# Attention with two matmul layers behind it: each pass over a pair of heads loads its own queries

## The chip, the cores and the metric

The kernel runs on one core of a Trainium2 chip. The metric is the device time of one execution in microseconds; the median of three runs before the change is 1149.49 us (1148.93 to 1151.54).

## The reference

Thirty-two heads (batch 4, 8 heads each) of 576 queries and keys with 64 features; every row of scores is cut at its maximum less tau before the exponent. Two layers over 2304 tokens follow, 512 to 2048 to 512 features each. All products are wanted in fp32; the weights arrive in 64 bits.

```python
scores = (q @ k.T) / 8
thresh = scores.max(-1) - tau
scores = where(scores >= thresh, scores, -1e9)
attn   = exp(scores - scores.max(-1))
x = (attn / (attn.sum(-1) + 1e-9)) @ v       # heads side by side: 2304 x 512
h = x @ w_in;  g = where(h >= 1, h, where(h <= -1, 0, (h + 1)**2 / 4));  y = g @ w_out
h = y @ w2_in; g = s * maximum(h, 0)**2 + b;                             out = g @ w2_out
```

## The kernel before

**Attention.** Two heads make a pair, and each pair is gone over twice. A unit is one pass: `half_` 0 takes the queries 0 to 255 in two tiles of 128, `half_` 1 the queries 256 to 575 in two tiles of 128 and a mixed tile, which holds the last 64 queries of both heads. There are 4 x 4 x 2 = 32 units. `prep` (line 389) loads queries and keys of the pair into a tile r (line 393, 128 rows of 1280 columns, 640 KB) and its values into vr (line 394), and scales all 640 columns of queries on POOL, VectorE or ACT (lines 397 to 399). Two tiles r and two vr take turns; the load for unit u+1 is added after the first query tile of the last part of unit u, and may start once the scores of unit u-1 have been computed.

For a query tile, `scores` (lines 424, 430) makes the products, VectorE finds the minimum of the negated scores (473), ACT takes the exponent (476), VectorE masks and sums (482), POOL or ACT normalises (518, 523), TensorE transposes in blocks (544, 558), ACT or VectorE evicts them to PT and PL (536, 537), and `av` (580, 581) multiplies by the values. Its result is split into a high and a low part, XH and XL (589, 592), and stored to xT (595). XH and XL exist twice; block q (256 tokens for even q, 320 for odd) uses number q % 2. The first 8 units compute the scores of one head at a time, the later ones of both heads together.

**The layers.** 16 slices f of 128 hidden features. A hidden tile is 12 matmuls (line 794), its outputs 12 more (837 in the attention stage, 880 and 914 afterwards). While attention runs, the layer's first slices are computed beside it for blocks 0 to 5: `FB[q]` slices for block q (`beside`, line 851). The rest of layer 1 and layer 2 follow when attention is over. Weights come in chunks of 128 x 256 (line 709, 256 KB each), and are turned from 64 bits into a high and a low part by ACT, VectorE and POOL (lines 712 to 725).

**The order of the work** is drawn by a planner, `Sched`, while the program is built. Every step is a task with the engines that can do it, their assumed durations, a priority, and keys that it reads and writes. `run` plays the tasks through: an engine that is free takes the ready task of the first priority; of two engines the one that is done sooner takes it, with a `PENALTY` on VectorE. A load is assumed to land after a time made of `DMA_ISSUE`, `DMA_RATE` and `DMA_LAG`. When TensorE has nothing ready, the planner puts in a fill matmul (line 986), whose product nobody reads. The order drawn so is fixed in the instruction queues; on the chip each engine and SP work through their queues in it, and wait on semaphores.

Attention steps get priorities (0, n) in the order in which they are added, shifted by `OFF[step]`; there are 304 numbers. Work of the layers comes behind, (1, n). The attention stage's weights stand among the attention steps, at W0 + WS * i, where i counts 20 parts (10 slices, each with an input and an output part).

```python
    f0, i = 0, 0
    for f1 in sorted(set(FB) | {F1}):
        for part in range(2):
            for f in range(f0, f1):
                weights(w1, f, (0, W0 + WS * i), (part,), 0)
                i += 1
        f0 = f1
```

In layer 1's last part the second layer's weights are loaded slice by slice as places come free, at least `PACE` slices apart.

Of the kernel before, what the change touches and what calls it, by code (L numbers as in the profile page):

```python
# [7 lines left out]
F32 = mybir.dt.float32  # L8
# [14 lines left out]
NWT = 4  # L23
TWO_PASS = 4

FB = [4, 8, 10, 10, 10, 10]
NA1 = len(FB)
PACE = 3
W0 = 40.0
WS = 5.75  # L30

WT0, WT = 0.0, 310.0

OFF = {"load": 0.0, "prep": 0, "qk": -6.0, "min": -3.0, "exp": -1.0, "mask": 0, "norm": 3.0, "trans": 3.58, "hi": 4.39, "av": 5.75, "xo": 0.0}
NSX, NSL, NR, NV = 4, 5, 2, 2
WARM = 9
# [5 lines left out]

QW, KW = 640, 640

ALONE = 6

APART = 8
DMA_ISSUE, DMA_RATE, DMA_LAG = 475, 360.0, 910.0
SCALE = 0.125

TINY, HUGE = 2.0 ** -15, 122880.0 - 2.0 ** -7

# [34 lines left out]
class Sched:  # L87
# [5 lines left out]
    CHANGE = 85.0  # L93
    PENALTY = {"dve": 1.5, "act": 0.3, "pool": 0.0}

# [53 lines left out]
    def run(self):  # L149
# [27 lines left out]
        while left:  # L177
# [4 lines left out]
            for d in batch:  # L182
                if d is None:
                    continue
                if d.group is not None:
                    d.group.left -= 1
                    if d.group.left == 0:
                        for b in d.group.banks:
                            bank_free[b] = None
                for s in d.succ:  # L190
                    s.preds.append((d.fn[0], now))
                    s.ready = max(s.ready, now)
                    s.npred -= 1
                    if s.npred == 0:
                        release(s)
            for e in engines:
# [7 lines left out]
                while q:  # L204
                    item = heapq.heappop(q)
                    t = self.tasks[item[1]]
                    if t.start is not None:
                        continue
                    g = t.group
                    if g is not None and g.banks is None:  # L210
                        pick = next((c for c in g.cands if all(bank_free.get(b) is None for b in c)), None)
                        if pick is None:
                            held.append(item)
                            continue
                        g.banks = pick
                        for b in pick:
                            bank_free[b] = g
# [24 lines left out]
                for item in held:  # L242
                    heapq.heappush(q, item)
                if e == "pe" and busy[e] <= now < self.fill_until:

                    b = next((b for b in self.fill_banks if bank_free.get(b) is None), None)
                    if b is not None:
# [3 lines left out]
                        t.fn = ("pe", self.fill_ns, self.fill(b))  # L251
                        bank_free[b] = t.group
                        busy[e] = array.run(now, self.fill_ns)
# [29 lines left out]
def pfast_ns(n):  # L283
    return 60 + 1.07 * n
# [20 lines left out]
def attention_then_ffn(tc, qk, v, tau, w1, w2, s2, b2, out):  # L305
# [77 lines left out]
    def at(pr, step):  # L383
        return pr[0], pr[1] + OFF[step]

    def load_const(key, dst, src, pr):
        add([("sp", DMA_ISSUE, lambda: nc.sync.dma_start(out=dst, in_=src.to_broadcast([128, 1])))], pr, w=[key], lag=512)

    def prep(u, b, pair):

        pr = prio_a()
        r, kr, vr, kvr = R[u % NR], ("R", u % NR), VR[u % NV], ("VR", u % NV)
# [4 lines left out]
        add([("pool", pfast_ns(QW), lambda: nc.gpsimd.tensor_scalar(out=q, in0=q, scalar1=-SCALE, scalar2=1.0, op0=ALU.mult, op1=ALU.mult)),  # L397
             ("dve", fast_ns(QW), lambda: nc.vector.tensor_scalar(out=q, in0=q, scalar1=-SCALE, scalar2=None, op0=ALU.mult), True),
             ("act", act_ns(QW), lambda: nc.scalar.activation(out=q, in_=q, func=AF.Copy, scale=-SCALE))],
            at(pr, "prep"), w=[kr])  # L400

    def both_tt(n, o, x, y, op):
# [6 lines left out]
    def scores(u, blk, hs):  # L409
# [6 lines left out]
        else:  # L416
            g = Group([(0, 1), (2, 3)] + [(6, 7)] * (u < ALONE))
        col = 0 if mixed else 128 + 128 * blk

        def qkmm():  # L420
            for x in range(2):
                if mixed:
                    k0 = QW + 64 + x * HS
                    nc.tensor.matmul(PS[g.banks[0]][:, x, 0:HS], r[:, col:col + 128], r[:, k0:k0 + HS], start=True, stop=True)  # L424
                    continue
                for i, h in enumerate(hs):
                    rows = slice(64 * h, 64 * h + 64)

                    k0 = QW + (0 if h else 64) + x * HS
                    nc.tensor.matmul(PS[g.banks[0] + 2 * i][:, x, 0:HS], r[rows, col:col + 128], r[rows, k0:k0 + HS], start=True, stop=True)  # L430
# [5 lines left out]
    def qtiles(u, blk):  # L436
# [94 lines left out]
        for x in range(nx):  # L531
            blocks_of_keys(pr, p, kp[2 * x], 0 if not x else S + 64, x, mixed, blk)
        last_keys(pr, p, kp[1], mixed, blk)

# [3 lines left out]

    def blocks_of_keys(pr, p, kp, c0, x, mixed, blk):
        g = Group([(4,), (5,)])  # L540
# [4 lines left out]

        add([("pe", 109 * 4, trans)], at(pr, "trans"), r=[kp], w=[("bank", g)], group=g)

# [4 lines left out]
        dst = PT[:, :, :, 512:S].rearrange("p s k c -> p k s c") if mixed else PT[:, x, :, blk * 128:blk * 128 + 128]  # L552
        evict(512, pr, [dst], src, [("bank", g)], [("PT", i, blk) for i in ((0, 1) if mixed else (x,))], g)

    def last_keys(pr, p, kp, mixed, blk):

        g = Group([(4,), (5,)])
        add([("pe", 109, lambda: nc.tensor.transpose(bank[g.banks[0]][:, 0:128], p[:, 512:640], ident))], at(pr, "trans"), r=[kp], w=[("bank", g)], group=g)  # L558

# [39 lines left out]

    units = [(b, pair, half_) for b in range(B) for half_ in ((0, 1) if b < TWO_PASS else (2,)) for pair in range(H // 2)]  # L600
    nxt = [0]

    def prep_next():
        if nxt[0] < len(units):
            prep(nxt[0], *units[nxt[0]][0:2])
            nxt[0] += 1
# [25 lines left out]
    def attention():  # L632
        prep_next()
        warm_up()
        load_const("tau", tau_c, tau, (0, 1.5))
        load_const("sb", s_c, s2, (0, 50))
# [185 lines left out]
    def a1_out(q, dm, slots):  # L822
# [4 lines left out]
        for half_ in range(2):  # L827
# [176 lines left out]
def _lay(inputs):  # L1004
    import numpy as np
    q, k, v = inputs["q"], inputs["k"], inputs["v"]
    qk = np.zeros((B, H, D, QW + KW), q.dtype)
    qt, kt = q.transpose(0, 1, 3, 2), k.transpose(0, 1, 3, 2)
    qk[:, 0::2, :, 0:64] = qt[:, 0::2, :, 512:]
    qk[:, 1::2, :, 64:128] = qt[:, 1::2, :, 512:]  # L1010
    qk[:, :, :, 128:QW] = qt[:, :, :, :512]
    qk[:, :, :, QW + 64:] = kt
    qk[:, 1::2, :, QW:QW + 64] = kt[:, 1::2, :, 512:]
    qk = qk.reshape(B, H // 2, 128, QW + KW)
    vp = np.zeros((B, H // 2, 128, 8 * D + 128), v.dtype)
# [36 lines left out]
```

## Time and profile before

| | us |
|---|---|
| median of three runs | 1149.49 |
| the profiled execution, its own time | 1148.21 |
| its span | 1146.4 |
| TensorE busy in the span | 1120.4 |
| VectorE, ACT, POOL busy | 621.4, 667.3, 542.8 |

The span runs from the first to the last instruction; the execution's own time holds 1.8 us around it. PE is TensorE's matmuls, PEld its weight loads, which overlap them. Matmuls are pipelined and their ends are modelled, so a busy PE need not be PE at its peak. The attention stage lies at 0 to 498 us, the rest of layer 1 up to 742 us, layer 2 behind it.

### The profile page before, as it was taken

The numbers are of one execution on the slowest core, as the hardware profiler recorded it, in microseconds if no ns is written. First come the engines' busy times: TensorE is split into PE (matmuls) and PEld (weight loads), VectorE is DVE, ScalarE is ACT, GpSimd is POOL, SyncE is SP. The second block draws the span as 40 slices with busy tenths as digits, with TensorE's granted clock in tenths as the row PEclk, the third lists the DMA queues.
The fourth block names the chain that finished last, engine by engine and source line by source line (L and its number), as shares of the span: only waits on it lengthen the run. The fifth ranks groups of instructions, "written<-read, shape, count | busy, mean of one in ns | idle before, by whom it ended". The sixth has DMA issues, their size and how long they took to land.

```text
span 1146.4 us, 21026 instructions
## 1 busy us (share of the span) xinstructions
PE 1120.4 (98%) x7608; PEld 976.1 (85%) x7608; DVE 621.4 (54%) x1519; ACT 667.3 (58%) x1538; POOL 542.8 (47%) x833
## 2 busy tenths in 40 slices
PE   9999989999999999999999999999999999999998
PEld 6667777777877788799999999999999999999997
DVE  6887877767756667548778875782111111111111
ACT  5887866757646656446665655565444444444443
POOL 4465565434434335347777765774323323233222
PEclk9999999999999999999999999999999999999999
DMA  4544634233222332145445765421001011000000
GB/s 161 171 129 151 185 112 128 70 104 118 94 69 88 110 103 74 53 138 165 146 155 178 234 193 177 135 87 38 19 19 37 3 36 38 1 19 20 1 19 19
DMA packets 66633, 108.86 MB, mean 95 GB/s; under 512 B 6368, under 2 KB 39648, under 8 KB 66528
## 3 DMA queue, kind: packets, MB, share of 16 engines
q1 hardware_dynamic: 66528, 107.50, 29.8%
q8 instruction: 60, 0.98, 0.3%
q14 instruction: 45, 0.37, 0.1%
HBM read 83.89 MB, written 23.59 MB: 94 GB/s over the span
## 4 chain that ended last, share of the span: by engine, by line
PE 82%; DMA 7%; DVE 4%; ACT 3%; POOL 1%; issue 1%; SPq 0%; ACTq 0%; DVEq 0%; POOLq 0%
PE ps L794 30%; PE ps L914 18%; PE ps L880 9%; PE ps L430 6%; PE ps L837 6%; PE ps L580 5%; PE ps L544 5%; DMA r<-in_qk_dram 4%; DMA st<-in_w_dram 3%; PE ps L581 2%; PE ps L424 1%; DVE p L482 1%; PE ps L558 1%; DVE hs L806 1%; PE ps L986 1%
## 5 line engine op out<-in xcount | busy, mean ns | idle before, releaser
L815 POOL TENSOR_TENSOR g<-hs,g 128x256 fp32r<-128x256 f32 (+1 forms) x272 | 214.0, 787 | 309.4 <-ACT g L814 287.7
L794 PE MATMUL ps<-xh,wh 128*128 128x256 f32 (+1 forms) x1088 | 317.8, 292 | 0.3 <-DVE hs L806 0.3
L794 PE MATMUL ps<-xl,wh 128*128 128x256 f32 (+1 forms) x1088 | 313.1, 288 | 0.0
L794 PE MATMUL ps<-xh,wl 128*128 128x256 f32 (+1 forms) x1088 | 312.9, 288 | 0.0
L812 DVE TENSOR_SCALAR hs<-c,s,b 128x256 f32<-128x256 f32 x144 | 65.2, 453 | 309.3 <-ACT c L811 309.3
L794 PEld LDWEIGHTS ps<-xh,wh 128*128 128x128 f32 x1088 | 206.0, 189 | 9.1 <-DVE stt L507 0.8
L794 PEld LDWEIGHTS ps<-xl,wh 128*128 128x128 f32 x1088 | 205.9, 189 | 6.2
L794 PEld LDWEIGHTS ps<-xh,wl 128*128 128x128 f32 x1088 | 205.8, 189 | 0.0
L914 PE MATMUL ps<-wh,g 128*128 128x512 f32 x576 | 203.2, 394 | 0.0
L814 ACT CAST g<-hs 128x256 fp32r<-128x256 f32 (+1 forms) x272 | 113.6, 418 | 94.9 <-DVE hs L812 62.8
L482 DVE SCALAR_TENSOR_TENSOR p<-ps,stt,e 128x576 f32<-128x576 f32 x144 | 115.5, 813 | 40.6 <-ACT e L476 21.4
L518 POOL TENSOR_SCALAR p<-p,stt 128x576 f32<-128x576 f32 (+1 forms) x124 | 98.2, 797 | 77.0 <-DVE stt L507 70.1
L809 ACT ACTIVATE hs<-ps 128x256 f32<-128x256 f32 x144 | 55.4, 385 | 132.3 <-PE ps L794 131.5
L473 DVE TENSOR_REDUCE stt<-ps 128x1 f32<-128x576 f32 x144 | 104.2, 750 | 48.7 <-PE ps L430 41.9
L403 POOL TENSOR_TENSOR wl<-wt,wh 128x256 fp32r<-128x256 f32 x128 | 101.5, 798 | 53.4 <-ACT wh L724 52.3
L914 PEld LDWEIGHTS ps<-wh,g 128*128 128x128 f32 x576 | 108.6, 189 | 19.5
L880 PE MATMUL ps<-g,wh 128*128 128x256 f32 (+1 forms) x608 | 122.7, 294 | 0.9 <-DVE ye L890 0.9
L476 ACT ACTIVATE e<-ps,stt 128x576 f32<-128x576 f32 x144 | 103.5, 744 | 32.9 <-DVE stt L473 30.7
L914 PE MATMUL ps<-wl,g 128*128 128x512 f32 x288 | 113.9, 395 | 0.0
L430 PE MATMUL ps<-r 64*128 64x288 f32 x512 | 98.3, 429 | 2.5 <-DVE p L482 2.3
L880 PEld LDWEIGHTS ps<-g,wh 128*128 128x128 f32 x608 | 97.3, 189 | 1.7 <-DVE ye L890 1.4
L804 ACT ACTIVATE c<-c,half 128x256 f32<-128x256 f32 (+1 forms) x128 | 68.6, 536 | 51.5 <-DVE c L802 49.5
(65 smaller groups left out, 1825.8 us busy)
## 6 DMA issues: line engine op xcount, KB each, us to landing
st<-in_w_dram SPq DMA_DIRECT2D x128, 256.0 KB, 3.6
r<-in_qk_dram SPq DMA_DIRECT2D x32, 640.0 KB, 4.4
vr<-in_v_dram SPq DMA_DIRECT2D x32, 320.0 KB, 3.3
xr<-xT SPq DMA_DIRECT2D x8, 640.0 KB, 6.1
xr<-y1T SPq DMA_DIRECT2D x9, 512.0 KB, 3.8
out_dram<-yo SPq DMA_DIRECT2D x18, 256.0 KB, 2.0
xr<-xT SPq DMA_DIRECT2D x8, 512.0 KB, 4.9
xT<-xh SPq DMA_DIRECT2D x16, 160.0 KB, 3.2
```

The lines of the kernel that those rows point to most:

```text
L403: return [("pool", pool_ns(n), lambda: nc.gpsimd.tensor_tensor(out=o(), in0=x(), in1=y(), op=op)), ("dve", dve_ns(n), lambda: nc.vector.te ...
L430: nc.tensor.matmul(PS[g.banks[0] + 2 * i][:, x, 0:HS], r[rows, col:col + 128], r[rows, k0:k0 + HS], start=True, stop=True)
L473: add([("dve", 665, lambda: nc.vector.tensor_reduce(out=nm[:, x:x + 1], in_=Sv(), axis=AX.XY, op=ALU.min))], at(pr, "min"), r=[kg], w=[ks[ ...
L476: add([("act", 624, lambda: nc.scalar.activation(out=ev, in_=Sv(), func=AF.Exp, bias=nm[:, x:x + 1], scale=-1.0))], at(pr, "exp"), r=[kg, ...
L482: nc.vector.scalar_tensor_tensor(out=p[:, x * S:x * S + S].rearrange("p (a c) -> p a c", a=2), in0=Sv(), scalar=nthr[:, x:x + 1], in1=ev, ...
L518: eng.tensor_scalar(out=p[:, o:o + w], in0=p[:, a:a + w], scalar1=rc[:, x:x + 1], scalar2=un[:, x:x + 1], op0=ALU.mult, op1=ALU.add)
L794: nc.tensor.matmul(o, a, x, start=(n == 0), stop=(n == 11))
L814: add([("act", act_ns(T), lambda: nc.scalar.copy(out=gh, in_=hs))], fp, r=[khs], w=kgh)
L815: add([("pool", pool_ns(T), lambda: nc.gpsimd.tensor_tensor(out=gl, in0=hs, in1=gh.bitcast(F32), op=ALU.subtract)), ("dve", dve_ns(T), lam ...
L837: nc.tensor.matmul(o, a[:, c], x, start=(f == 0 and n == 0), stop=(f == nf - 1 and n == 2))
L880: nc.tensor.matmul(o, a[:, c], x, start=(f == f0 and n == 0), stop=(f == f1 - 1 and n == 2))
L914: nc.tensor.matmul(o, x[:, c], a[:, 512:1024], start=(f == 0 and n == 0), stop=(f == NF - 1 and n == 2))
```

## The change

Each pass loads only its queries and the keys. In DRAM the pair lies as queries 0 to 255, keys, then the mixed tile's and the other queries; pass 0 takes the columns 0 to 895 (448 KB), pass 1 the columns 256 to 1279 (512 KB), and scales 256 or 384 columns of queries. Three tiles r of 1024 columns take turns instead of two of 1280; the values, in a function of their own and with a priority of their own, stay with two tiles. With that the attention has 336 priority numbers. `TWO_PASS` goes, which already named all batches, and `AHEAD = 1` adds no load.

In the planner: loads are assumed to land later, a bank counts as free only when TensorE could have heard of it, VectorE's penalty is 2.0, scores are drawn earlier and the normalisation too. Transposes of the first six units wait in the plan for their place in PT or PL, and the output sums beside attention follow one another. Fewer slices stand beside blocks 0 and 1, weights come 8 apart, the second layer's 5.

```diff
-FB = [4, 8, 10, 10, 10, 10]
+FB = [3, 7, 10, 10, 10, 10]
-PACE = 3
+PACE = 5
-WS = 5.75
+WS = 8.0
-OFF = {"load": 0.0, "prep": 0, "qk": -6.0, "min": -3.0, "exp": -1.0, "mask": 0, "norm": 3.0, ...}
+OFF = {"load": 0.0, "prep": 0, "qk": -8.0, "min": -3.0, "exp": -1.0, "mask": 0, "norm": 0.0, ...}
-NSX, NSL, NR, NV = 4, 5, 2, 2
+NSX, NSL, NR, NV = 4, 5, 3, 2
-QW, KW = 640, 640
+KW = 640
+PASS = ((0, 256 + KW), (256, KW + 384))
+KEYS, QUERIES = (256, 0), ((0, 256), (KW, KW + 384))
-DMA_ISSUE, DMA_RATE, DMA_LAG = 475, 360.0, 910.0
+DMA_ISSUE, DMA_RATE, DMA_LAG = 475, 350.0, 2500.0
-    PENALTY = {"dve": 1.5, "act": 0.3, "pool": 0.0}
+    PENALTY = {"dve": 2.0, "act": 0.3, "pool": 0.0}
...
+                        heard = now + self.HOP.get((d.fn[0], "pe"), 0)
                         for b in d.group.banks:
-                            bank_free[b] = None
+                            bank_free[b] = heard
...
-                        dma_free = max(dma_free, now + 1125.0) + t.lag / DMA_RATE
+                        dma_free = max(dma_free, now + 1400.0) + t.lag / DMA_RATE
...
-    R = [ap_.tile([128, QW + KW], F32, name=f"r{i}") for i in range(NR)]
+    R = [ap_.tile([128, 384 + KW], F32, name=f"r{i}") for i in range(NR)]
...
-    def prep(u, b, pair):
+    def prep(u, b, pair, half_):
-        add([("sp", DMA_ISSUE, lambda: nc.sync.dma_start(out=r, in_=qk[b, pair]))], at(pr, "load"), w=[kr], lag=128 * (QW + KW) * 4)
-        add([("sp", DMA_ISSUE, lambda: nc.sync.dma_start(out=vr, in_=v[b, pair]))],
-            at(pr, "load"), w=[kvr], lag=128 * 640 * 4)
-        q = r[:, 0:QW]
+        c0, n = PASS[half_]
+        add([("sp", DMA_ISSUE, lambda: nc.sync.dma_start(out=r[:, 0:n], in_=qk[b, pair][:, c0:c0 + n]))], at(pr, "load"), w=[kr], lag=128 * n * 4)
+        q0, q1 = QUERIES[half_]
+        q, w = r[:, q0:q1], q1 - q0
...
+    def values(u, b, pair, half_):
+        add([("sp", DMA_ISSUE, lambda: nc.sync.dma_start(out=VR[u % NV], in_=v[b, pair]))],
+            at(prio_a(), "load"), w=[("VR", u % NV)], lag=128 * 640 * 4)
...
-        add([("pe", 109 * 4, trans)], at(pr, "trans"), r=[kp], w=[("bank", g)], group=g)
+        kt = [("PT", i, blk) for i in ((0, 1) if mixed else (x,))]
+        add([("pe", 109 * 4, trans)], at(pr, "trans"), r=[kp], w=[("bank", g)] + kt * (u < ALONE), group=g)
...
                 if part == (half_ == 1) and t == blks[0]:
-                    prep_next()
+                    next_of(prep)
+                    next_of(values)
...
-            add([("pe", 3 * len(fs) * mm_ns(T), mm, "r")], pr, r=rd, w=[kg], group=g)
+            add([("pe", 3 * len(fs) * mm_ns(T), mm, "r")], pr, r=rd, w=[kg, "sums"], group=g)
```

## Rows read from the trace of the kernel before

**Rows 1.** The page: engines (busy us, share, instructions), the chain by engine.

```profile
PE 1120.4 (98%) x7608; PEld 976.1 (85%) x7608; DVE 621.4 (54%) x1519; ACT 667.3 (58%) x1538; POOL 542.8 (47%) x833
...
PE 82%; DMA 7%; DVE 4%; ACT 3%; POOL 1%; issue 1%; SPq 0%; ACTq 0%; DVEq 0%; POOLq 0%
```

**Rows 2.** Busy time by stage: length, each engine's busy us, clock, DMA.

```profile
20.00:220.00 200.00, 187.36 (x1214) 141.20 (x1214) 159.71 (x440) 151.27 (x322) 113.88 (x193) 0.99 0.45 137
220.00:498.00 278.00, 272.29 (x1917) 217.08 (x1914) 181.06 (x466) 167.45 (x338) 108.52 (x171) 1.00 0.28 87
498.00:742.00 244.00, 243.05 (x1845) 242.29 (x1844) 183.54 (x406) 145.12 (x371) 169.60 (x251) 1.00 0.56 176
```

**Rows 3.** Fills (line 986): two stages; sums around r loads, around weight loads.

```profile
20.00:220.00 200.00, 12.80 (x82) 11.03 (x82) 0.99 0.45 137
220.00:498.00 278.00, 0.00 (x0) 0.00 (x0) 1.00 0.28 87
...
sum 48.00, PE 1.77 PEld 1.53; mean PE 0.35 PEld 0.31
...
sum 22.00, PE 5.87 PEld 5.08; mean PE 2.94 PEld 2.54
```

**Rows 4.** Busy time: two stretches; sums around r (twice) and weights (last).

```profile
40.00:60.00 20.00, 18.60 (x97) 11.88 (x96) 15.60 (x46) 15.42 (x31) 9.71 (x20) 0.91 0.51 154
...
420.00:440.00 20.00, 20.00 (x140) 16.86 (x138) 16.19 (x42) 14.44 (x31) 9.68 (x15) 1.00 0.21 64
...
sum 48.00, PE 42.07 PEld 32.29 DVE 35.29 ACT 30.77 POOL 25.66; mean PE 8.41 PEld 6.46 DVE 7.06 ACT 6.15 POOL 5.13
...
sum 30.00, PE 26.34 PEld 22.71 DVE 19.85 ACT 18.79 POOL 9.40; mean PE 8.78 PEld 7.57 DVE 6.62 ACT 6.26 POOL 3.13
...
sum 22.00, PE 19.99 PEld 16.07 DVE 18.70 ACT 16.37 POOL 12.21; mean PE 9.99 PEld 8.03 DVE 9.35 ACT 8.18 POOL 6.11
```

**Rows 5.** The chain of waits by line, 20 to 220 us and 220 to 500.

```profile
by line: PE ps L430 15.6%; DMA r<-in_qk_dram 14.9%; PE ps L544 10.1%; PE ps L794 9.1%; PE ps L580 8.4%; PE ps L837 6.7%; DMA st<-in_w_dram 6.2%; PE ps L424 2.8%; PE ps L581 2.7%; issue 2.7%; DVE p L482 2.3%; PE ps L558 2.2%; PE ps L986 1.4%
...
by line: PE ps L837 18.5%; PE ps L580 13.8%; PE ps L794 12.8%; PE ps L430 11.8%; PE ps L544 11.1%; DMA r<-in_qk_dram 6.2%; PE ps L581 4.5%; PE ps L424 3.1%; DVE p L482 2.6%; DVE stt L473 2.5%; PE ps L558 2.2%; issue 2.0%; ACT e L476 1.7%; D
```

**Rows 6.** Pieces of the chain: start us, us, what.

```profile
40.27 6.72 DMA r<-in_qk_dram
...
49.37 1.51 PE ps L430 x4
...
76.81 1.44 PE ps L794 x12
...
100.26 4.12 DMA st<-in_w_dram
...
126.80 1.76 PE ps L794 x12
```

**Rows 7.** The page's DMA issues: KB each, median us to landing.

```profile
r<-in_qk_dram SPq DMA_DIRECT2D x32, 640.0 KB, 4.4
vr<-in_v_dram SPq DMA_DIRECT2D x32, 320.0 KB, 3.3
```

**Rows 8.** Groups by form, 0 to 498 us: busy us, mean ns of one.

```profile
L712 ACT ACTIVATE wt<-st 128x256 f32<-128x256 f32 x40 | 17.5, 442 | 11.5 <-DMA st<-in_w_dram 6.3 <-POOL wl L403 5.1
...
L399 ACT ACTIVATE r<-r 128x640 f32<-128x640 f32 x18 | 13.3, 737 | 16.6 <-DMA r<-in_qk_dram 16.5
...
L537 DVE COPY pl<-ps 128x128 f32<-128x128 f32 x6 | 1.7, 285 | 2.4 <-PE ps L558 2.4
...
L537 DVE COPY pl<-ps 64x64 f32<-64x64 f32 x4 | 0.9, 216 | 0.0
```

**Rows 9.** SP's waits, 0 to 498 us: us in total, times, longest.

```profile
SPq L394 <- PE ps L581: 142.0, 30, 14.4
```

**Rows 10.** Weight loads of attention, block 2's hidden matmuls: ns, first and last start us.

```profile
L709 SPq DMA_DIRECT2D st<-in_w_dram x36: 327/328/439, 26.2 to 176.1; - x36
...
L794 PE MATMUL ps<-xh,wh x40: 277/283/386, 192.1 to 225.9; 128*128 128x256 f32 x40
```

More of the change, by code (lines that the diff above doesn't have):

```diff
@@ L23 @@
 NWT = 4
-TWO_PASS = 4
-FB = [4, 8, 10, 10, 10, 10]
+FB = [3, 7, 10, 10, 10, 10]
 NA1 = len(FB)
-PACE = 3
+PACE = 5
 W0 = 40.0
-WS = 5.75
+WS = 8.0
 WT0, WT = 0.0, 310.0
-OFF = {"load": 0.0, "prep": 0, "qk": -6.0, "min": -3.0, "exp": -1.0, "mask": 0, "norm": 3.0, "trans": 3.58, "hi": 4.39, "av": 5.75, "xo": 0.0}
-NSX, NSL, NR, NV = 4, 5, 2, 2
+OFF = {"load": 0.0, "prep": 0, "qk": -8.0, "min": -3.0, "exp": -1.0, "mask": 0, "norm": 0.0, "trans": 3.58, "hi": 4.39, "av": 5.75, "xo": 0.0}
+NSX, NSL, NR, NV = 4, 5, 3, 2
+AHEAD = 1
 WARM = 9
@@ L41 @@
 NGA, NGL = F1 + 1, 6
-QW, KW = 640, 640
+KW = 640
+PASS = ((0, 256 + KW), (256, KW + 384))
+KEYS, QUERIES = (256, 0), ((0, 256), (KW, KW + 384))
 ALONE = 6
 APART = 8
-DMA_ISSUE, DMA_RATE, DMA_LAG = 475, 360.0, 910.0
+DMA_ISSUE, DMA_RATE, DMA_LAG = 475, 350.0, 2500.0
 SCALE = 0.125
 TINY, HUGE = 2.0 ** -15, 122880.0 - 2.0 ** -7
+HELD = float("inf")
 class Group:
@@ L187, in run @@
                     if d.group.left == 0:
+                        heard = now + self.HOP.get((d.fn[0], "pe"), 0)
                         for b in d.group.banks:
-                            bank_free[b] = None
+                            bank_free[b] = heard
+                        seq += 1
+                        heapq.heappush(events, (heard, seq, None))
                 for s in d.succ:
@@ L210, in run @@
                     if g is not None and g.banks is None:
-                        pick = next((c for c in g.cands if all(bank_free.get(b) is None for b in c)), None)
+                        pick = next((c for c in g.cands if all(bank_free.get(b, 0.0) <= now for b in c)), None)
                         if pick is None:
@@ L216, in run @@
                         for b in pick:
-                            bank_free[b] = g
+                            bank_free[b] = HELD
                     t.fn = next(a for a in t.alts if a[0] == e)
@@ L244, in run @@
                 if e == "pe" and busy[e] <= now < self.fill_until:
-                    b = next((b for b in self.fill_banks if bank_free.get(b) is None), None)
+                    b = next((b for b in self.fill_banks if bank_free.get(b, 0.0) <= now), None)
                     if b is not None:
@@ L251, in run @@
                         t.fn = ("pe", self.fill_ns, self.fill(b))
-                        bank_free[b] = t.group
+                        bank_free[b] = HELD
                         busy[e] = array.run(now, self.fill_ns)
@@ L387, in load_const @@
         add([("sp", DMA_ISSUE, lambda: nc.sync.dma_start(out=dst, in_=src.to_broadcast([128, 1])))], pr, w=[key], lag=512)
-    def prep(u, b, pair):
+    def prep(u, b, pair, half_):
         pr = prio_a()
-        r, kr, vr, kvr = R[u % NR], ("R", u % NR), VR[u % NV], ("VR", u % NV)
-        add([("sp", DMA_ISSUE, lambda: nc.sync.dma_start(out=r, in_=qk[b, pair]))], at(pr, "load"), w=[kr], lag=128 * (QW + KW) * 4)
-        add([("sp", DMA_ISSUE, lambda: nc.sync.dma_start(out=vr, in_=v[b, pair]))],
-            at(pr, "load"), w=[kvr], lag=128 * 640 * 4)
-        q = r[:, 0:QW]
-        add([("pool", pfast_ns(QW), lambda: nc.gpsimd.tensor_scalar(out=q, in0=q, scalar1=-SCALE, scalar2=1.0, op0=ALU.mult, op1=ALU.mult)),
-             ("dve", fast_ns(QW), lambda: nc.vector.tensor_scalar(out=q, in0=q, scalar1=-SCALE, scalar2=None, op0=ALU.mult), True),
-             ("act", act_ns(QW), lambda: nc.scalar.activation(out=q, in_=q, func=AF.Copy, scale=-SCALE))],
+        r, kr = R[u % NR], ("R", u % NR)
+        c0, n = PASS[half_]
+        add([("sp", DMA_ISSUE, lambda: nc.sync.dma_start(out=r[:, 0:n], in_=qk[b, pair][:, c0:c0 + n]))], at(pr, "load"), w=[kr], lag=128 * n * 4)
+        q0, q1 = QUERIES[half_]
+        q, w = r[:, q0:q1], q1 - q0
+        add([("pool", pfast_ns(w), lambda: nc.gpsimd.tensor_scalar(out=q, in0=q, scalar1=-SCALE, scalar2=1.0, op0=ALU.mult, op1=ALU.mult)),
+             ("dve", fast_ns(w), lambda: nc.vector.tensor_scalar(out=q, in0=q, scalar1=-SCALE, scalar2=None, op0=ALU.mult), True),
+             ("act", act_ns(w), lambda: nc.scalar.activation(out=q, in_=q, func=AF.Copy, scale=-SCALE))],
             at(pr, "prep"), w=[kr])
+    def values(u, b, pair, half_):
+        add([("sp", DMA_ISSUE, lambda: nc.sync.dma_start(out=VR[u % NV], in_=v[b, pair]))],
+            at(prio_a(), "load"), w=[("VR", u % NV)], lag=128 * 640 * 4)
     def both_tt(n, o, x, y, op):
@@ L417, in scores @@
             g = Group([(0, 1), (2, 3)] + [(6, 7)] * (u < ALONE))
-        col = 0 if mixed else 128 + 128 * blk
+        half_ = units[u][2]
+        col, keys = KW if mixed else 128 * blk if not half_ else KW + 128 + 128 * (blk - 2), KEYS[half_]
         def qkmm():
@@ L422, in qkmm @@
                 if mixed:
-                    k0 = QW + 64 + x * HS
+                    k0 = keys + 64 + x * HS
                     nc.tensor.matmul(PS[g.banks[0]][:, x, 0:HS], r[:, col:col + 128], r[:, k0:k0 + HS], start=True, stop=True)
@@ L427, in qkmm @@
                     rows = slice(64 * h, 64 * h + 64)
-                    k0 = QW + (0 if h else 64) + x * HS
+                    k0 = keys + (0 if h else 64) + x * HS
                     nc.tensor.matmul(PS[g.banks[0] + 2 * i][:, x, 0:HS], r[rows, col:col + 128], r[rows, k0:k0 + HS], start=True, stop=True)
@@ L531, in qtiles @@
         for x in range(nx):
-            blocks_of_keys(pr, p, kp[2 * x], 0 if not x else S + 64, x, mixed, blk)
-        last_keys(pr, p, kp[1], mixed, blk)
+            blocks_of_keys(u, pr, p, kp[2 * x], 0 if not x else S + 64, x, mixed, blk)
+        last_keys(u, pr, p, kp[1], mixed, blk)
     def evict(n, pr, dst, src, r, w, g):
@@ L537, in evict, with blocks_of_keys @@
              ("dve", dve_ns(n), lambda: [nc.vector.tensor_copy(out=a, in_=b) for a, b in zip(dst, src())])], at(pr, "hi"), r=r, w=w, group=g)
-    def blocks_of_keys(pr, p, kp, c0, x, mixed, blk):
+    def blocks_of_keys(u, pr, p, kp, c0, x, mixed, blk):
         g = Group([(4,), (5,)])
@@ L552, in blocks_of_keys, with last_keys @@
         dst = PT[:, :, :, 512:S].rearrange("p s k c -> p k s c") if mixed else PT[:, x, :, blk * 128:blk * 128 + 128]
-        evict(512, pr, [dst], src, [("bank", g)], [("PT", i, blk) for i in ((0, 1) if mixed else (x,))], g)
-    def last_keys(pr, p, kp, mixed, blk):
+        evict(512, pr, [dst], src, [("bank", g)], kt, g)
+    def last_keys(u, pr, p, kp, mixed, blk):
         g = Group([(4,), (5,)])
-        add([("pe", 109, lambda: nc.tensor.transpose(bank[g.banks[0]][:, 0:128], p[:, 512:640], ident))], at(pr, "trans"), r=[kp], w=[("bank", g)], group=g)
+        add([("pe", 109, lambda: nc.tensor.transpose(bank[g.banks[0]][:, 0:128], p[:, 512:640], ident))], at(pr, "trans"), r=[kp], w=[("bank", g)] + [("PL", blk)] * (u < ALONE), group=g)
         def src():
@@ L596, in av, with next_of @@
                 r=[k], w=[("xT", q, pair, x)], lag=128 * n * 4)
[L600 to L606, printed above, removed]
+    units = [(b, pair, half_) for b in range(B) for half_ in range(2) for pair in range(H // 2)]
+    nxt = {prep: 0, values: 0}
+    def next_of(step):
+        if nxt[step] < len(units):
+            step(nxt[step], *units[nxt[step]])
+            nxt[step] += 1
     def pair_of_heads(u):
@@ L632, in attention @@
     def attention():
-        prep_next()
+        next_of(prep)
         warm_up()
+        for _ in range(1, AHEAD):
+            next_of(prep)
+        next_of(values)
         load_const("tau", tau_c, tau, (0, 1.5))
@@ L1006, in _lay @@
     q, k, v = inputs["q"], inputs["k"], inputs["v"]
-    qk = np.zeros((B, H, D, QW + KW), q.dtype)
     qt, kt = q.transpose(0, 1, 3, 2), k.transpose(0, 1, 3, 2)
[L1009 to L1014, printed above, removed]
+    qk = np.zeros((B, H, D, 640 + KW), q.dtype)
+    qk[..., 0:256] = qt[..., 0:256]
+    qk[..., 320:256 + KW] = kt
+    qk[:, 1::2, :, 256:320] = kt[:, 1::2, :, 512:]
+    for x in range(2):
+        qk[:, x::2, :, 256 + KW + 64 * x:320 + KW + 64 * x] = qt[:, x::2, :, 512:]
+    qk[..., 384 + KW:] = qt[..., 256:512]
+    qk = qk.reshape(B, H // 2, 128, 640 + KW)
     vp = np.zeros((B, H // 2, 128, 8 * D + 128), v.dtype)
```

## The prediction

> **What bounds the kernel now.** I read the page's engine table first, then the chain of waits, then busy time by stage, and last the chain and the stretches around the two kinds of load that stand in it. The page shows a TensorE that is busy 98% of the span, and a chain of which 82% is TensorE and 7% DMA [rows 1]. That share is an average over three stages, so it has to be split [rows 2]. From 498 us on (the rest of layer 1, then layer 2) TensorE is dense: 243.05 of 244 us in 498 to 742, with weight loads back to back at 242.29. Nothing that this change does can win more than the 0.95 us of idle time there. What can be won lies in the attention stage.
>
> From 20 to 220 us TensorE is busy 187.36 of 200 us, and 12.80 us of that are fill matmuls of line 986, which compute nothing [rows 2, 3]. For a few microseconds the clock also sat at 1.2 GHz: 40 to 60 us has a mean grant of 0.91, so 20 x 0.09 = 1.8 us of full-speed time are missing [rows 4]. The visible reserve is 12.64 + 12.80 + 1.8 = 27.2 us. From 220 to 498 us there are no fills, and the idle time is 278 - 272.29 = 5.7 us. Together: 32.9 us, and a change of order alone cannot give much more than this unless TensorE also runs its busy time more densely (the second rival).
>
> The chain says what is late there. In 20 to 220 us loads of r take 14.9% (29.8 us) and loads of weights 6.2% (12.4 us); in 220 to 500 us r takes 6.2% (17.4 us) [rows 5]. One of the eight long r pieces shows the pattern: the load is issued at 40.27 us, lands 6.72 us later, is scaled at once, and scores, exponent and mask follow one another until the next scores at 49.37 us [rows 6]. With two r tiles the load for unit u+1 can start only after the last scores of unit u-1, so its landing is needed almost as soon as it comes.
>
> **The change part by part.**
>
> *Three r tiles, smaller loads.* With three tiles the load for u+1 needs only the scores of u-2 to be over, one whole unit sooner. A unit lasts about 478/32 = 15 us in the stage; the longest r piece is 6.72 us. So the load should be landed and scaled before its scores are due, and the r pieces leave the chain. That is worth not their 47 us but what TensorE loses beside them. In five stretches around the r pieces of 20 to 220 us (48 us in all) it is busy 42.07 us, of which 1.77 us fills: 5.93 + 1.77 = 7.7 us. The lost clock of 1.8 us is in the first of them. In three stretches of the later part 30 - 26.34 = 3.7 us are idle [rows 3, 4]. Sum 13.2 us. The ends: nothing, if the same time is lost to the next wait, and 13.2 us; I take all of it, because in each stretch the chain has no DMA but r ahead of the next TensorE piece. VectorE is late next: it is busy 159.71 of 200 us [rows 2], so a stage shorter by 15 us would load it to 86%, which it can bear.
>
> The bytes matter less. The load falls from 640 KB to 448 or 512 KB. Trace medians are 4.4 us for 640 KB and 3.3 us for 320 KB [rows 7], so by a straight line the new loads take 3.7 and 4.0 us, about 0.5 us less. Scaling takes 737 ns for 640 columns on ACT, and an ACT pass over 256 columns takes 442 ns [rows 8]: about 0.25 us less in each of 32 units, 8 us of ACT and POOL in all. Both lie ahead of need once the third tile is there, so I cost them at nothing; if the cover is gone, it is 0.75 us for each of the eight pieces, 6 us of gain that the first term already holds.
>
> On SP's queue the r issue moves ahead of the v load, which stays bound to two tiles. That v load is where SP sits longest, 142.0 us over 30 waits, up to 14.4 us [rows 9], with stores of x and weight loads behind it. The plan issues a load when its tile is free in the plan, so r now stands ahead of that wait, and the number of issues is the same. I cost it at nothing; r behind v would take the first term back.
>
> *Weights further apart, fewer hidden tiles beside the first two blocks.* The attention's chain waits for weights at 100.26 us for 4.12 us [rows 6]; in 94 to 106 and 117 to 127 us TensorE loses 22 - 19.99 = 2.0 us idle and 5.87 us in fills [rows 3, 4]. WS = 8 puts the last of 20 weight parts at priority 40 + 19 x 8 = 192 instead of 149, and attention gets the engines first. A block that needs fewer f beside it (3 and 7 instead of 4 and 8) needs fewer weights early: block 0 waits for parts up to priority 80 before and after. The gain lies between 7.9 us and a loss (the slower rival below). I take half, 4 us.
>
> The two f that move go to the dense stage, where they are not hidden: 2 x 1.44 us for 256 tokens and 2 x 1.76 us for 320 (12 matmuls for the hidden tile, 12 for its outputs) = 6.4 us [rows 6]. Where the attention stage is bound by TensorE it gets shorter by as much; where fills stand in their place it does not. From 0 to 6.4 us, I take 3.2 us of loss.
>
> *The plan's constants.* Transfers planned longer (lag 2500 ns for 910), banks counted as free only after TensorE has heard of it, transposes of the first six units that wait in the plan for PT, scores drawn earlier (-8 for -6), normalisation earlier: all these change only the order within each queue. The reserve beside neither load is 32.9 - 13.2 - 7.9 = 11.8 us. Order can win from it or lose as much; I take a quarter, 3 us of gain. VectorE's higher penalty finds little to move: VectorE has 10 of the small evictions of line 537, 0.22 to 0.29 us each [rows 8], and nothing of the normalisations. PACE = 5 spreads the second layer's weights in a stage with 0.95 us of idle time; nothing.
>
> **Sum.** -13.2 - 4 + 3.2 - 3 = -17.0 us, against the profiled execution's own 1148.2 us (span 1146.4 us, 1.8 us around it): 1131.2 us. The median of the runs is 1.3 us above that execution, so 1132.5 us.
>
> The Trainium skill (Trainium Kernel Development and Optimization, Performance Expectations) says that matmul busy time is a bad measure of how full TensorE is, and that the share of weight loads is a good one. The rows bear it out in part: where TensorE is busy all the time in both, weight loads fill 99% in 498 to 742 us, but 84% in 420 to 440 us of attention [rows 2, 4]. By that rule the reserve is larger than my 32.9 us, and the second rival is the time it would give.
>
> **The rivals.**
>
> 1. *Hidden anyway.* r leaves the chain, but TensorE had other work meanwhile and the same tiles are only run in another order; the next chain is VectorE's mask and ACT's eviction of PT. For it: of the 48 us around the r pieces TensorE is busy 42.07 us, and no row has TensorE wait for r by itself. Against it: VectorE and ACT are only 80% and 76% busy there [rows 2]. Then the r term is about a quarter, 3.3 us, and the moved f cost 3.2 us: 1149 us.
>
> 2. *A deeper reserve.* If the attention stage gets as dense as 420 to 440 us, which has 16.86 us of weight loads in 20 us [rows 4], then 141.20 us of loads need 167.5 us instead of 200, and 217.08 us need 257.5 us instead of 278: 53 us of reserve. Two thirds of it is 35 us: 1114 us. For it: fills and unpaired weights go first. Against: the stretches do different work, and part of the gap may belong to matmuls that keep the array longer for each weight load.
>
> 3. *Slower: weights come too late for block 2.* Its hidden tiles f = 7 to 9 need the last six parts. Before, the last weight is issued at 176.1 us, and that block's ten tiles run from 192.1 to 225.9 us, the last three near its end [rows 10]. The attention counts 304 steps before and 336 after, so 149 of 304 becomes 192 of 336, and 176 us becomes about 176 x 0.571/0.491 = 205 us. Landing and six passes later that is just in time at the old pace, and late at a faster one. If three tiles are late, TensorE fills for 3 x 2 x 1.44 = 8.6 us, the values of unit 16 on wait for XH behind them, the moved f cost their full 6.4 us, and half of the r term (6.6 us) is lost again with them: +8.4 us, 1158 us. It decides if the last weight of the attention stage is issued later than about 210 us.
>
> **How the numbers follow.** Forecast 0.46 (its own range 1122 to 1144 us: all of the weights' and the order's terms, or neither and the moved f in full), hidden anyway 0.20, deeper reserve 0.15, slower 0.19. About 0.2% (2.3 us) is what a measurement of this kernel can tell from no change. Faster: forecast, deeper reserve and a third of the first rival, 0.68; within 0.2%: 0.13; slower 0.19. The range reaches into the deeper reserve and past no change: 1114 to 1154 us.
>
> **What would show it.** r pieces of the chain in 20 to 500 us under 10 us instead of 47 (step one); engines no longer waiting for r when they scale it; fills after 20 us well under 12.80 us (weights); attention ended some 22 us sooner, at about 476 us, and the dense stage longer by some 6 us. Wrong: r gone from the chain and attention ending after 490 us (first rival); the last weight after 210 us, with fills beyond 200 us (third).

## The result, and the profile after

The changed kernel takes 1121.24 us in the median of four runs (1120.51 to 1121.81), the kernel before 1150.51 us beside it: a ratio of 0.9743, 95% interval 0.9723 to 0.9764, or 29.3 us less. Forecast were 1132.5 us and 17 us less. Direction and outer range (1114 to 1154 us) held; the gain is 1.7 times the forecast one, and the time lies just under the forecast's own range of 1122 to 1144 us. Two of the ten runs of E1 below, 1156.4 and 1160.3 us at a mean granted clock of 0.98, count as slow and are left out of its numbers.

The page of the changed kernel, engines and chain by engine. DMA, 7% of the chain before [rows 1], is gone from it:

```profile
PE 1109.0 (99%) x7608; PEld 971.8 (87%) x7608; DVE 608.7 (54%) x1450; ACT 663.9 (59%) x1539; POOL 550.1 (49%) x901
...
PE 94%; DVE 3%; ACT 2%; POOL 1%; issue 1%; ACTq 0%; POOLq 0%; DVEq 0%
```

Busy time of the changed kernel by stage, with columns as in [rows 2], which it answers:

```profile
20.00:220.00 200.00, 198.39 (x1341) 150.62 (x1340) 175.77 (x456) 160.13 (x348) 127.43 (x231) 1.00 0.46 136
220.00:478.00 258.00, 257.84 (x1859) 211.73 (x1858) 161.28 (x391) 157.50 (x324) 104.15 (x196) 1.00 0.29 87
```

In 20 to 220 us TensorE's idle time falls from 12.64 to 1.61 us, later in the stage from 5.7 to 0.2 us, and the lost clock is back. VectorE, 80% busy there before, is at 88% now. The fills hardly fall. This is their sum (line 1009 now) over 20 to 220 us; [rows 3] had 12.80:

```profile
sum 200.00, PE 10.59 PEld 9.59; mean PE 5.30 PEld 4.79
```

The chain by line, 20 to 220 us, to be read beside [rows 5]. Lines stand in the order of their shares, and no load is among them:

```profile
by line: PE ps L447 19.3%; PE ps L599 13.7%; PE ps L561 11.7%; PE ps L860 10.1%; PE ps L817 6.4%; PE ps L600 4.5%; PE ps L1009 3.9%; PE ps L441 2.9%; issue 2.9%; DVE p L499 2.8%; DVE stt L490 2.7%; PE ps L577 2.2%; ACT e L493 2.1%; ACT pt L
```

Engines that use r waited for its load 45.0 us in 24 places before; in the changed kernel (second fence) 7.7 us in 3. Under it stands the landing time of r in us:

```profile
  DMA r<-in_qk_dram: 45.0, 24
```

```profile
  DMA r<-in_qk_dram: 7.7, 3
...
DMA to landing us min/median/max: 3.3/3.9/7.8
```

Two value products mark the time: that of unit 7, the end of the first 8 units, and that of unit 31, the end of attention. Start and length, of the kernel before and then of the changed one:

```profile
123.54 0.81 PE L581 MATMUL ps<-pl,vr 128*128 128x320 f32 x2
...
496.85 0.81 PE L581 MATMUL ps<-pl,vr 128*128 128x320 f32 x2
```

```profile
110.16 0.81 PE L600 MATMUL ps<-pl,vr 128*128 128x320 f32 x2
...
464.93 0.81 PE L600 MATMUL ps<-pl,vr 128*128 128x320 f32 x2
```

Attention ends 31.9 us sooner; what follows it takes 4.2 us more (the span is 27.7 us shorter). Busy time from the start to the end of attention, before and then after:

```profile
0.00:497.66 497.66, 477.31 (x3218) 372.13 (x3219) 351.00 (x930) 326.85 (x672) 230.49 (x386) 1.00 0.36 111
...
0.00:465.74 465.74, 461.51 (x3194) 364.00 (x3195) 343.14 (x861) 323.13 (x677) 237.62 (x450) 1.00 0.36 107
```

Of the 31.9 us, 16.1 us are idle time of TensorE (20.35 us before, 4.23 us after) and 1.0 us fills, counted from the start. Matmuls of the layer make up 3.9 us: 24 fewer run before attention ends, not the 48 of the two moved slices, because the changed kernel has more hidden tiles of the next stage done by then. With the 1.8 us of clock that is 22.8 us. About 9 us lie inside TensorE's busy time, where no row gives their cause.

### The profile page after: what moved, and what is told of

It reads as the page before. It is cut to its first block, busy times and chain, and to the rows that moved or that the text cites. A ratio compares the mean times of both kernels' runs of the same rounds, so it can differ in the third digit from the quotient of the medians.

```text
span 1118.7 us, 21095 instructions
## 1 busy us (share of the span) xinstructions
PE 1109.0 (99%) x7608; PEld 971.8 (87%) x7608; DVE 608.7 (54%) x1450; ACT 663.9 (59%) x1539; POOL 550.1 (49%) x901
## 4 chain that ended last, share of the span: by engine, by line
PE 94%; DVE 3%; ACT 2%; POOL 1%; issue 1%; ACTq 0%; POOLq 0%; DVEq 0%
PE ps L817 35%; PE ps L937 18%; PE ps L903 11%; PE ps L447 7%; PE ps L860 7%; PE ps L599 6%; PE ps L561 5%; PE ps L600 2%; PE ps L1009 1%; PE ps L441 1%; PE ps L577 1%; DVE p L499 1%; DVE stt L490 1%; ACT e L493 1%; ACT pt L553 0%
## 5 line engine op out<-in xcount | busy, mean ns | idle before, releaser
L903 PE MATMUL ps<-g,wh 128*128 128x256 f32 (+1 forms) x624 | 126.6, 295 | 1.2 <-DVE ye L913 0.6
L535 POOL TENSOR_SCALAR p<-p,stt 128x576 f32<-128x576 f32 (+1 forms) x118 | 93.7, 798 | 27.1 <-DVE stt L524 18.8
L827 ACT ACTIVATE c<-c,half 128x320 f32<-128x320 f32 (+1 forms) x128 | 68.7, 537 | 57.7 <-DVE c L825 56.7
L903 PEld LDWEIGHTS ps<-g,wh 128*128 128x128 f32 x624 | 100.0, 189 | 2.4 <-DVE ye L913 1.4
L447 PE MATMUL ps<-r 64*128 64x288 f32 x512 | 95.6, 428 | 1.3 <-DVE p L499 1.3
```

The lines of the kernel that those rows point to most:

```text
L535: eng.tensor_scalar(out=p[:, o:o + w], in0=p[:, a:a + w], scalar1=rc[:, x:x + 1], scalar2=un[:, x:x + 1], op0=ALU.mult, op1=ALU.add)
L903: nc.tensor.matmul(o, a[:, c], x, start=(f == f0 and n == 0), stop=(f == f1 - 1 and n == 2))
```

## The experiments

Each kernel was timed beside the kernel before on its chip: E1 to E4 on one (before 1150.9 us), E5 to E8 on a second (1147.7 us), E9 to E12 on a third (1147.2 us, 1143.5 to 1154.7). Differences from the changed kernel are taken to 1121.2 us, which E4, all but the same kernel, also shows beside E1 to E3. For E5 to E12 they cross chips, so the ratio to the kernel before stands with each; taken by the ratios, these differences would be 1 to 6 us larger (E6 17, E7 12, E8 6 us). Part of that is the clock, of which the kernel before lost different amounts on the three chips. The last column is an estimate for it: the median of each run's time multiplied by its mean granted clock, so the time without the lost clock. By it the kernel before takes 1145.8, 1144.6 and 1144.3 us on the three chips, and E4, the changed kernel again, 1121.

| | median us (lowest to highest) | ratio, 95% interval | time x clock, us |
|---|---|---|---|
| E1 loads alone | 1139.66 (1138.03 to 1145.76) | 0.9903, 0.9882 to 0.9925 | 1138 |
| E2 all but the loads | 1125.20 (1124.71 to 1125.76) | 0.9767, 0.9738 to 0.9796 | 1124 |
| E3 two tiles | 1123.04 (1122.38 to 1131.50) | 0.9765, 0.9721 to 0.9810 | 1122 |
| E4 nudge | 1121.27 (1120.74 to 1122.12) | 0.9734, 0.9699 to 0.9769 | 1121 |
| E5 landing time alone | 1135.88 (1135.68 to 1136.61) | 0.9899, 0.9875 to 0.9922 | 1136 |
| E6 old landing time | 1134.92 (1131.76 to 1140.57) | 0.9894, 0.9856 to 0.9932 | 1129 |
| E7 old slices and spacing | 1130.40 (1129.92 to 1130.94) | 0.9850, 0.9830 to 0.9869 | 1130 |
| E8 old offsets | 1124.16 (1123.69 to 1124.61) | 0.9795, 0.9776 to 0.9815 | 1124 |
| E9 old slices | 1130.65 (1130.04 to 1138.97) | 0.9855, 0.9800 to 0.9910 | 1130 |
| E10 old spacing | 1135.97 (1135.25 to 1139.48) | 0.9892, 0.9859 to 0.9925 | 1134 |
| E11 old landing time, weights | 1137.19 (1126.20 to 1137.84) | 0.9891, 0.9827 to 0.9955 | 1125 |
| E12 old landing time, the rest | 1132.86 (1131.98 to 1141.65) | 0.9893, 0.9834 to 0.9952 | 1132 |

**E1, the loads alone.** `PASS`, `values`, `NR = 3`; every other constant as before.

```diff
-NSX, NSL, NR, NV = 4, 5, 2, 2
+NSX, NSL, NR, NV = 4, 5, 3, 2
...
+        c0, n = PASS[half_]
```

> Only the loads are changed: own queries for each pass, three r tiles, values apart; slices beside attention, weight spacing and every constant of the plan are as before. Theory (the r loads that stood on the chain cost 13 of the 29 us): 1137 us, r under 10 us of the chain between 20 and 500 us. Rival (the order drawn by the new constants gives nearly all): 1147 us or more, TensorE still idle some 15 us in 20 to 220 us, with r gone from the chain.

11.2 us, near the theory's 13. The chain by line in 20 to 220 us of this kernel: r is left with at most 1.9% (and 3.4% of 220 to 480 us), and the weight loads, 6.2% before [rows 5], stand in its place with 13.1%, 26 us. Engines that use r still wait for it 37.9 us in 27 places (second fence): the new loads alone take r nearly off the chain, but not out of the waits.

```profile
by line: PE ps L447 14.4%; PE ps L599 13.5%; DMA st<-in_w_dram 13.1%; PE ps L561 9.1%; PE ps L817 8.0%; PE ps L860 7.4%; PE ps L600 4.1%; PE ps L1009 3.2%; issue 2.3%; DVE p L499 2.2%; DVE stt L490 2.2%; POOL p L535 1.9%; DMA r<-in_qk_dram 
```

```profile
  DMA r<-in_qk_dram: 37.9, 27
```

**E2, all but the loads.** The kernel before with the new plan, slices and spacing.

```diff
-FB = [4, 8, 10, 10, 10, 10]
+FB = [3, 7, 10, 10, 10, 10]
...
 NSX, NSL, NR, NV = 4, 5, 2, 2
...
-DMA_ISSUE, DMA_RATE, DMA_LAG = 475, 360.0, 910.0
+DMA_ISSUE, DMA_RATE, DMA_LAG = 475, 350.0, 2500.0
...
```

> The kernel before with everything of the change except the loads: new constants of the plan, slices and spacing of the weights, but two r tiles of 1280 columns and all 640 query columns scaled in each unit. Theory: the loads' 13 us are missing, 1134 us, r back on the chain with 30 us or more. Rival (order gives nearly all): 1124 us.

The rival held: 1125.2 us, the interval far from the theory's 1134. The loads are as long as before and two tiles take turns, yet the page's chain by engine has no DMA (first fence). TensorE in 20 to 220 us is about as full as in the changed kernel (busy sum, and the engines that wait for r, in us and times):

```profile
PE 94%; DVE 3%; ACT 2%; issue 1%; POOL 0%; ACTq 0%; POOLq 0%
```

```profile
sum 200.00, PE 198.11 PEld 149.67 DVE 174.31 ACT 165.24 POOL 125.74; mean PE 99.06 PEld 74.84 DVE 87.15 ACT 82.62 POOL 62.87
```

```profile
  DMA r<-in_qk_dram: 9.8, 7
```

**E3, two tiles** in the changed kernel.

```diff
-NSX, NSL, NR, NV = 4, 5, 3, 2
+NSX, NSL, NR, NV = 4, 5, 2, 2
```

> The changed kernel with two r tiles instead of three (NR = 2), the smaller loads kept. Theory (the third tile, not the bytes, takes r off the chain): 1133 us, r on the chain with 25 us or more. Rival (smaller loads and a plan that knows the load's length are enough): 1123 us.

The rival held again: the third tile is worth 1.8 us under the new plan, with the smaller loads kept. The chain by engine of this kernel's page has no DMA:

```profile
PE 97%; ACT 1%; DVE 1%; issue 0%; POOL 0%; ACTq 0%; POOLq 0%; DVEq 0%
```

**E4, a nudge:** `DMA_RATE` 351 for 350.

> The changed kernel with an assumed load rate of 351 for 350, a difference without meaning of its own. It measures what any redrawing of the order is worth. Theory (the gain has causes): within 3 us of 1121 us. Rival (orders scatter by their own luck): more than 6 us away, in which case no difference under that says anything.

The time is the same, but this says little about the luck of an order. In the traces of the two kernels TensorE's queue is the same in all 7608 matmuls, and no queue differs before 650 us, long after attention; only the end of layer 1 and what follows were redrawn. So the rival was not tested where the gain lies. How far orders of the attention stage scatter by luck is not known, and differences of a few microseconds (E3, E8, parts of E7, E9 and E10) may hold some of it.

**E5, the landing time alone,** in the kernel before.

```diff
-DMA_ISSUE, DMA_RATE, DMA_LAG = 475, 360.0, 910.0
+DMA_ISSUE, DMA_RATE, DMA_LAG = 475, 350.0, 2500.0
...
-                        dma_free = max(dma_free, now + 1125.0) + t.lag / DMA_RATE
+                        dma_free = max(dma_free, now + 1400.0) + t.lag / DMA_RATE
```

> The kernel before with nothing changed but the landing time that the plan assumes for a load (lag 2500 for 910, floor 1400 for 1125, rate 350 for 360). Theory now (the plan put work that needs a load ahead of its landing, and the queues then stood; a truer time mends that without a faster load): 1134 us or less, r under 10 us of the chain from 20 to 500 us although the loads are as long as before. Rival (the other edits of the plan, bank times, penalty and offsets, do it): within 4 us of the kernel before.

Three numbers in the planner give 11.8 us, about 9 of them by time x clock. The page's chain by engine has no DMA, and r is waited for 9.2 us in 4 places instead of 45.0 in 24 (second fence). But TensorE's loss has changed its form: idle time in 20 to 220 us falls to 3.9 us, and fills rise from 12.80 to 17.96 us (third fence, the fills' sum). Where TensorE has nothing to do, the plan now knows it and puts in a fill.

```profile
PE 95%; DVE 2%; ACT 2%; issue 1%; POOL 0%; ACTq 0%; DVEq 0%; POOLq 0%
```

```profile
  DMA r<-in_qk_dram: 9.2, 4
```

```profile
sum 200.00, PE 17.96 PEld 15.96; mean PE 8.98 PEld 7.98
```

**E6, the old landing time** in the changed kernel (E5's edit, the other way).

> The changed kernel with the old assumed landing time (lag 910, floor 1125, rate 360). Theory (the truer landing time carries most of the gain): 1130 us or more, weight loads and r back on the chain. Rival (early loads make the assumption idle, or other edits carry it): under 1125 us.

13.7 us slower, as the theory had it; about 6 us of that are the clock. The two runs at a mean grant of 0.998 took 1131.8 and 1132.8 us, the two at 0.989 and 0.991 took 1140.6 and 1137.1 us; time x clock is 8 us above the changed kernel. The chain in 20 to 220 us shows weight loads that come too late for the plan, three r tiles or not; engines that use r wait for it 25.1 us in 17 places as well:

```profile
by line: PE ps L447 15.5%; DMA st<-in_w_dram 11.9%; PE ps L561 9.1%; PE ps L599 7.9%; PE ps L817 7.9%; issue 4.2%; DVE p L499 4.1%; PE ps L860 3.1%; ACT e L493 2.8%; PE ps L600 2.4%; POOL p L535 2.4%; DVE stt L490 2.4%; PE ps L1009 2.1%; DM
```

**E7, the old slices and spacing** in the changed kernel.

```diff
-FB = [3, 7, 10, 10, 10, 10]
+FB = [4, 8, 10, 10, 10, 10]
...
-PACE = 5
+PACE = 3
...
-WS = 8.0
+WS = 5.75
```

> The changed kernel with the old slices and spacings (FB 4 and 8, WS 5.75, PACE 3). Theory (TensorE is full in the attention stage, so where two slices are computed is nearly free, and weights 8 apart save some): 1124 us. Rival (the 4 us that I gave the spacing and the 3 us of the moved slices were both wrong, as weights further apart are what makes VectorE free early): 1130 us.

9.2 us slower, the rival's 1130. The first 8 units' last value product starts at 119.57 us instead of 110.16: a loss as large as the whole stands there already, and the fills of 20 to 220 us rise from 10.59 by 8.05 us, nearly all of it:

```profile
119.57 0.81 PE L600 MATMUL ps<-pl,vr 128*128 128x320 f32 x2
```

```profile
sum 200.00, PE 18.64 PEld 16.74; mean PE 9.32 PEld 8.37
```

**E8, the old offsets:** `"qk": -6.0` and `"norm": 3.0` in the changed kernel.

> The changed kernel with the old offsets of scores and normalisation (-6 and 3). Theory (the offsets are a small part): 1124 us. Rival (scores drawn earlier keep TensorE and VectorE apart and carry much of the gain): 1130 us or more, with VectorE waiting for scores more than the 40 us of now.

2.9 us slower, as the theory had it. Whether luck of the order does as much was not tested.

**E9 and E10, slices and spacing apart:** `FB` alone, then `WS` alone, set back.

> The changed kernel with 4 and 8 slices beside blocks 0 and 1 instead of 3 and 7, spacing kept at 8. Theory (the two slices beside the first blocks need weights before VectorE has finished them, so TensorE fills and block 0 of attention is held up): 1128 us, with the first eight units ending at 117 us or later instead of 111. Rival (the spacing carries the 9 us): 1122 us.

> The changed kernel with weights 5.75 apart instead of 8, slices kept at 3 and 7. Theory (the slices carry the larger part of the 9 us): 1124 us. Rival (weights that crowd the first units cost most of it): 1129 us, the first eight units ending at 118 us or later.

E9 costs 9.4 us; its theory was near. E10 costs 14.7 us, more than either side expected, and more than both edits with PACE together (E7). The fills of E10 in 20 to 220 us are 12.6 us above those of the changed kernel (fence). Also, r is back on its chain with 3.3% of 20 to 220 us, 6.6 us, in spite of three tiles and the truer landing time; in E7 the page's chain has no DMA.

```profile
sum 200.00, PE 23.20 PEld 20.93; mean PE 11.60 PEld 10.47
```

So these edits do not add up, and what one is worth can be told only with the rest given. Whether that is because each fits the others or because orders scatter, no run tells. E9's profiled run was its longest and is taken up under hardware.

**E11 and E12, whose landing time:** the old one for weight loads alone, then for all other loads and stores.

```diff
...
+                        old = t.lag == 128 * 8 * WC        # E12: !=
+                        dma_free = max(dma_free, now + (1125.0 if old else 1400.0)) + t.lag / (360.0 if old else DMA_RATE)
+                        end = dma_free + (910.0 if old else DMA_LAG)
```

> The changed kernel with the old assumed landing time for the weight loads alone; queries, values and stores keep the new one. Theory (of the 14 us that the old time costs here most is the weights, whose loads stand on the chain of that run with 24 us): 1131 us. Rival (r, v and the stores carry it): 1123 us.

> The changed kernel with the old assumed landing time for all loads and stores but the weights. Theory (three tiles make r early whatever the plan believes): 1124 us. Rival (r is late again): 1130 us or more, r on the chain with 10 us or more.

E12 refutes my theory: with three tiles and short loads, but a plan that believes in the old landing time, the kernel is 11.6 us slower, r is waited for 29.2 us in 21 places (fence), and it stands on the chain with 2.3% of 20 to 220 us and 2.6% of 220 to 480 us, 11 us:

```profile
  DMA r<-in_qk_dram: 29.2, 21
```

E11's four runs fall apart by the clock: three, at a mean grant of 0.989, took 1137 us, the fourth, at 1.000, took 1126.2 us. The profiled one, of the former, has weight loads as 15.2% of the chain of 20 to 130 us and half the clock for part of it (below). So the weights' old landing time costs some 5 us in the one run that kept the clock, and 16 us in the three that lost some of it. The theory's 1131 us is met by neither; at the full clock the larger part is the rest's (E12).

## Why the prediction came out as it did

**What bounds the kernel: right.** The gain lies in the attention stage, and there in TensorE's idle time. The reserve that I could see was 32.9 us, from 20 us on; 20.6 us of it were won (16.6 us idle time, 2.2 us fills, 1.8 us clock), and about 9 us inside the busy time that I had not counted. By the Trainium skill (Trainium Kernel Development and Optimization, Performance Expectations) the share of weight loads shows more than the busy time, and it did show a reserve beyond mine; the share in 20 to 220 us rose from 71% to 75%, though, not to the 84% from which I had worked out 53 us. The time lies between the forecast (1132.5 us) and the deeper reserve (1114 us), nearer to the latter.

**The range: held, in part by luck.** The terms of the sum were off in both directions, as the next paragraphs say, and the errors partly cancelled. The forecast's own range does not follow from the terms that it names either: all of the weights' and the order's terms with the sum's 3.2 us for the slices give about 1120 us, neither of them and the slices in full 1143 us, where it says 1122 and 1144.

**The third tile: right in size alone, wrong as the cause.** I gave the loads 13.2 us because their pieces stood on the chain. Alone they bring 11.2 us (E1), and r all but leaves the chain. But on top of the rest they bring 4.0 us (E2), the third tile 1.8 us (E3), and without the truer landing time r comes back on the chain even with three tiles (E12). A load that stands on the chain can be mended from two ends: make it earlier, or stop planning work for a time at which it has not landed. The step said "the r pieces leave the chain" because of the third tile, and the second end does it without (E2, E5).

**"The plan's constants ... I take a quarter, 3 us of gain": the step that failed.** The assumed landing times are one of the two largest parts that the runs show (slices and spacing are the other), and all numbers for it stood in the code and in the profile. Before, the plan let r land after 1125 + 655360 / 360 + 910 ns = 3.86 us and a weight chunk after 1125 + 262144 / 360 + 910 ns = 2.76 us, with medians of 4.4 us [rows 7] and 3.6 us measured on the page. No chunk landed that early: the fastest took 2.9 us. In the trace before, all 40 weight loads of the attention stage took longer than these sums, 31 of 32 loads of v (2.95 us by the plan) and 27 of 32 loads of r; in the changed kernel it is 8, 2 and 5. So nearly every load was late by plan, and in queues of fixed order one late operand holds up all that stands behind it. After, the plan says 5.2 or 5.4 us for r and 4.65 us for weights, above the medians of 4.1, 3.8 and 3.6 us. That one edit is worth 11.8 us alone and 13.7 us in the whole (E5, E6), 8 to 9 us either way by time x clock, against the 3 us that I gave to all constants together. I treated it as one of several that "change only the order", and priced order by the reserve left over from the loads; but the loss beside the loads was this edit's too.

**Weights and slices: too small, and the slices with the wrong sign.** I had 4 us of gain for the spacing and 3.2 us of loss for the two moved slices, 0.8 us of gain in all. Together they are worth 9.2 us (E7), and the slices by themselves are a gain (E9). The dense stage did become longer, by 4.2 us where I had up to 6.4, and attention shorter by more: the first 8 units end 9.4 us sooner, and 8.05 us of fills go. As I read it, fewer and later weights in the first units leave VectorE to attention: it is 84% busy in 20 to 120 us with the old slices and spacing and 92% with the new ones. That this is the cause was not shown by itself.

**The slower rival: refuted at its own point.** It was to decide at 210 us. The last weight of the attention stage is issued at about 164 us, sooner than the 176 us of before, in spite of higher priority numbers. "Hidden anyway" said 1149 us and is refuted by E1's 1139.7 us.

**Signs foretold.** r off the chain, waits for r gone, attention ended at 466 us where I said 476, what follows it longer by 4.2 us where I said 6: all seen. Not seen: fills well under 12.80 us. They fell by 2.2 us, because the truer plan turns idle time into fills (E5) while slices and spacing take fills away (E7). And the clock: I counted the 1.8 us that the profiled execution had lost, at a mean grant of 0.998. On the first chip the kernel before had 0.995 in the median of 13 runs, so some 5 us of the 29.3 us are clock that the changed kernel, at 0.999 to 1.000, does not lose.

**Left open.** E5 to E8 undo landing time, slices and offsets for 13.7, 9.2 and 2.9 us, and E2 leaves 4.0 us for the loads; the sum of 29.8 us is close to 29.3, but E9 and E10 show that such parts do not add, the lost clock is in some of them, and they cross chips, so I don't read it as a division. The new bank times, the keys for PT and the sums, the penalty and PACE were not run apart. Why the spacing alone costs more than spacing and slices together was not found, and how much orders of the attention stage differ by luck was not measured.

## What to carry to other kernels

Where a planner fixes the order of in-order queues, compare each duration that it assumes with the measured one before anything else: here a plan that expected weights before the fastest of them had landed, and r and v earlier than most of theirs, cost 8 to 14 us against one that expected them a microsecond or more after the median. No value between or above was run. Count what the array loses as idle time, fills and lost clock together, since a better plan first turns one into the other. And undo an edit in the new kernel as well as doing it alone in the old one: r's loads were worth 11.2 us the one way and 4.0 us the other. When a nudge is to measure the luck of an order, look first whether it changed the order in the stage that counts.

## What the runs showed of the hardware

The clock can be halved for a long stretch while TensorE looks busy. E9's profiled execution took 1138.97 us, its four others 1130.0 to 1130.7 us. Busy time and granted clock (the third number from the end) in it, from 10 to 35 us:

```profile
10.00:15.00 5.00, 4.27 (x21) 2.79 (x19) 4.77 (x11) 3.41 (x6) 2.66 (x9) 0.99 0.56 183
15.00:20.00 5.00, 5.00 (x13) 2.88 (x12) 2.87 (x9) 1.92 (x5) 2.98 (x9) 0.50 0.24 79
20.00:35.00 15.00, 14.62 (x47) 8.62 (x46) 8.22 (x22) 6.91 (x13) 5.46 (x12) 0.50 0.15 53
```

The grant is 0.50, 1.2 GHz, with TensorE busy 14.62 of 15 us. Just before the fall it was busy 4.27 us of 5, and the changed kernel, at the full 2.4 GHz throughout, was busy 4.26 us of its 5 at that place. So this row does not tell the two apart. The fall cost some 8.5 us against E9's four other runs; E11's profiled run, too, has a grant of 0.50 from 15 us on.

Most of the spread from run to run is this clock. For every run the record has the mean granted clock, and time x clock brings the runs of one kernel together: E11's from 11.6 us apart to 1.7, E12's from 9.7 to 2.7, E9's from 8.9 to 2.5, E6's from 8.8 to 3.6, and those of the kernel before on the third chip from 11.1 to 4.5. The runs of E2, E5, E7 and E8, with no DMA on their chain, were all granted 0.999 or 1.000 and lie within 1.1 us; the kernel before, E1, E6, E11 and E12, with DMA there, had runs at 0.992 or less. But E3 and E9, without DMA, had one run each at 0.990, so a chain with waits for DMA goes with a lost clock here and is not shown to be its only cause.
